# A linear-attention and feed-forward kernel: w3 @ w_out by row blocks, the weight loads moved and reordered, the last block made four units

## The chip, the core and the metric

The kernel runs on one core of a Trainium2 chip. A core has a matrix engine (TensorE, PE in the profile), a vector engine (VectorE, DVE), a scalar engine (ScalarE, ACT), GpSimd (POOL) and SyncE (SP), which issues transfers; 16 DMA engines move the data. Each engine works through its own queue in order. The metric is the device time of one execution in microseconds. Chances of "faster" and "slower" are meant against the median of the runs before.

## What is computed

```python
def _attn_ref(r, k, v, w, u):            # batch 4, heads 8, sequence 768, head_dim 48
    state = zeros((B, H, D, D)); y = zeros_like(r)
    for t in range(S):
        kt, vt, rt, wt = k[:, :, t], v[:, :, t], r[:, :, t], w[:, :, t]
        cur = einsum('bhd,bhe->bhde', u[None] * kt, vt)
        y[:, :, t] = einsum('bhd,bhde->bhe', rt, state + cur)
        state = wt[:, :, :, None] * state + einsum('bhd,bhe->bhde', kt, vt)
    return y

def _moe_ref(x, w1, w2, w3, w_out):      # x: y as 3072 tokens x 384; d_ff 1024
    h = (x @ w1) * (x @ w2) @ w3
    return h @ w_out
```

All inputs and the output are float32 in memory; the kernel multiplies in bfloat16. Since nothing stands between w3 and w_out, it forms w34 = w3 @ w_out (1024 x 384) once and uses that for the output.

## The kernel before

The 3072 tokens are 24 chunks (units) of 128: 4 batches with 6 chunks each. A chunk takes four loads of 192 KB (w, k, r, v, on SP's queue, line 237) and then the attention steps of `att(n)` (line 269): `ln` and the two cumulative sums `cs`, `ex`, the scaled k and r (`krt`), their transposes (`tr`, copied by `trs`), the chunk's contribution to the state (`kv`, `ts`, `pc`, `sbd`, `s_f`), the score matrix `m` with its two masked copies (`mb0`, `mb1`), `y`, and the diagonal term by way of `uk1`, `uk2`, `ds`, `yd`. `yb` adds the two, `yt` transposes and `xt` writes the chunk into `xT` of its block. `vb` casts v to bfloat16 on POOL. A trace names tiles, so that `uk1` and `uk2` both show as uk, `mb` as mbf, `ln` as lw.

The feed-forward works on blocks of chunks (`BLOCKS`, line 177): two blocks of two, four of four, and two of two at the end. For each of 8 column blocks `fi`, `a` and `b` (line 438) multiply w1 and w2 with xT, `as` copies a out of PSUM on ScalarE and `ab` multiplies it with b on VectorE. `o` (line 468) multiplies the product with w34, `os` copies it out, `st` stores. w34 comes from two steps: 8 times `wt` (8 transposes of w3, copied into the full transposed `w3T`, line 490) and then 8 times `wm` (line 500), which needs all eight copies; `wc` casts each result.

Every step is given to `Plan` (line 14) with its engine, an assumed length, its needs and the buffers that it takes and frees. `Plan._pass` walks through assumed time: of the ready steps the one that can start first on its engine goes next, and `rank` decides ties. The result is a fixed order, in which the instructions are issued; on the chip each engine keeps that order, whatever the real durations are. The plan knows loads of chunks at 1000 rows per us, and at 85 rows per us in the windows that it gives to weight loads. A "need" between a POOL load and an earlier POOL step is no wait on the chip, only a place in the queue.

Weights are loaded by POOL: w1 and w2 after `ld_r0`, w3 and w_out after `ld_v3` in the plan. Attention is put into the list of steps ahead of the feed-forward parts by a running count (`lead, every = 3, 4.1`).

Of the kernel before, what the change touches and what calls it, by code (L numbers as in the profile page):

```python
# [13 lines left out]
class Plan:  # L14
# [21 lines left out]
    def _pass(self, windows):  # L36
        end, eng_free, taken, owner, released = {}, {}, {}, {}, {}
        left = dict(self.steps)
        waiting = {n: sum(d not in end for d in s["needs"]) for n, s in left.items()}
        users = {}  # L40
        for n, s in left.items():
            for d in s["needs"]:
                users.setdefault(d, []).append(n)
        frees = {}
        for n, s in left.items():
            for o in s["free"]:
                frees[o] = frees.get(o, 0) + 1
        freed = {}
        ready = {n for n, c in waiting.items() if c == 0}
        order, ring, ring_free, big_free, new_windows, start = [], [], 0.0, 0.0, [], {}  # L50
        while left:
            best = {}
            for n in ready:
                s = left[n]
                t = eng_free.get(s["eng"], 0.0)
                for d in s["needs"]:
                    t = max(t, end[d] + (self.HOP if self.steps[d]["eng"] != s["eng"] else 0.0))
                ok = True
                for b in s["take"]:
                    i = taken.get(b, 0) - self.count[b]  # L60
                    if i >= 0:
                        o = owner[b, i]
                        if freed.get(o, 0) < frees[o]:
                            ok = False
                            break
                        t = max(t, released[o] + self.HOP)
                if not ok:
                    continue
                if s["rows"] and len(ring) >= 8:
                    t = max(t, ring[-8])  # L70
                best.setdefault(s["eng"], []).append((t, s["rank"], n))
            assert best, ("stuck", sorted(left)[:20])
            picks = []
            for e, c in best.items():
                t0 = min(c)[0]
                picks.append(min((max(t, t0), r, n) for t, r, n in c if t <= t0 + 1e-9))
            t, _, n = min(picks)
            s = left.pop(n)
            ready.discard(n)
            order.append(n)  # L80
            start[n] = t
            eng_free[s["eng"]] = t + s["length"]
            if s["rows"]:
                at, rows = max(t + 0.3, ring_free), s["rows"]
                while rows > 1e-6:
                    w = next((x for x in windows if x[0] <= at < x[1]), None)
                    nxt = w[1] if w else min([x[0] for x in windows if x[0] > at] + [1e9])
                    rate = 85.0 if w else 1000.0
                    d = min(rows / rate, nxt - at)
                    rows -= d * rate  # L90
                    at += d
                ring_free = at
                end[n] = at + 1.9
                ring.append(end[n])
            elif s["big"]:
                at = max(t + 2.0, big_free)
                big_free = at + s["big"]
                new_windows.append((at, big_free))
                end[n] = big_free + 1.5
            else:  # L100
                end[n] = t + s["length"] + s["lag"]
            for b in s["take"]:
                owner[b, taken.get(b, 0)] = n
                taken[b] = taken.get(b, 0) + 1
            for o in s["free"]:
                freed[o] = freed.get(o, 0) + 1
                released[o] = max(released.get(o, 0.0), end[n])
            for u in users.get(n, ()):
                waiting[u] -= 1
                if waiting[u] == 0:  # L110
                    ready.add(u)
        return order, new_windows, start, end
# [28 lines left out]
def kernel(  # L141
# [23 lines left out]
    P = 128  # L165
# [8 lines left out]
    TB = 512  # L174
    NU = B * NC
    NIN = 8
    BLOCKS = [(0, 2), (2, 4)] + [(n, n + 4) for n in range(4, NU - 4, 4)] + [(NU - 4, NU - 2), (NU - 2, NU)]
    NB = len(BLOCKS)

    consts = ctx.enter_context(tc.tile_pool(name="consts", bufs=1))  # L180
    wpool = ctx.enter_context(tc.tile_pool(name="weights", bufs=1))
# [32 lines left out]
    w2_bf = wpool.tile([P, DI, DFF], BF)  # L214
    w3_bf = wpool.tile([P, FI, DFF], BF)
    wo_bf = wpool.tile([P, FI, DM], BF)
    w3T = wpool.tile([P, FI, DFF], BF)
    w34 = wpool.tile([P, FI, DM], BF)

    NS = 3  # L220
# [6 lines left out]
    for i in range(NS):  # L227
# [2 lines left out]

    plan = Plan()
    plan.buffers(w_in=NIN, kr_in=NIN, v_in=NIN, lw=NS, krt=NS, sbd=NS, v_bf=3, e_sb=2, uk=2, ds=2, yd=3,
                 trs=2, mbf=2, pc=2, ts=2, s_f=2, y_bf=2, a_sb=3, o_sb=3, xT=3, abT=3, f=3, t=2, m=1, y=1)
    T = {}


    def load(n):
# [25 lines left out]

    def load_w(name, dst, ap, size, needs):
        plan.add(name, "POOL", 0.9, lambda: pool.dma_start(dst, ap.rearrange("(i p) f -> p i f", p=P)),
                 needs=needs, big=size, rank=-1)


    def att(n):
# [138 lines left out]
        if not last:  # L408
# [15 lines left out]
        A(f"uk2{n}", "POOL", 1.05, uk2, needs=[f"uk1{n}", f"ld_r{n}"], free=[f"ld_k{n}"])  # L424
        A(f"ds{n}", "DVE", 0.5, ds, needs=[f"uk2{n}"], take=["ds"], free=[f"uk1{n}"])
        A(f"yd{n}", "POOL", 0.82, yd, needs=[f"ds{n}", f"vb{n}"], take=["yd"], free=[f"ds{n}"])
        A(f"y{n}", "PE", 0.42, y, needs=[f"mb1{n}"] + ([f"sbd{n - 1}"] if c else []), take=["y"], lag=0.2,
          free=[f"mb0{n}", f"trs{n}", f"vb{n}"] + ([f"sbd{n - 1}"] if c else []))
        A(f"yb{n}", "DVE", 0.5, yb, needs=[f"y{n}", f"yd{n}"], take=["y_bf"], free=[f"y{n}", f"yd{n}"])
        A(f"yt{n}", "PE", 0.18, yt, needs=[f"yb{n}"], take=["t"], lag=0.2, free=[f"yb{n}"])  # L430
# [7 lines left out]
    def ffn_ab(j, fi):  # L438
# [14 lines left out]
        def mul():  # L453
# [3 lines left out]

        A = plan.add
        xs = [f"xt{n}" for n in range(lo, hi)]
        A(f"a{j}.{fi}", "PE", 0.65 * s, lambda: half("a", w1_bf), needs=xs + ["w1"], take=["f"], lag=0.2)  # L460
        A(f"b{j}.{fi}", "PE", 0.65 * s, lambda: half("b", w2_bf), needs=xs + ["w2", f"a{j}.{fi}"], take=["f"],
          lag=0.2, free=[f"xt{lo}"] if fi == FI - 1 else [])
        A(f"as{j}.{fi}", "ACT", 0.1 + 0.43 * s, a_cp, needs=[f"a{j}.{fi}"], take=["a_sb"], free=[f"a{j}.{fi}"])
        A(f"ab{j}.{fi}", "DVE", 0.1 + 0.53 * s, mul,
          needs=[f"as{j}.{fi}", f"b{j}.{fi}"] + ([f"ab{j}.0"] if fi else []), take=[] if fi else ["abT"],
          free=[f"as{j}.{fi}", f"b{j}.{fi}"])

    def ffn_out(j, t_):
        lo, hi = BLOCKS[j]
# [11 lines left out]
        def st():  # L481
# [2 lines left out]
        A = plan.add  # L484
        A(f"o{j}.{t_}", "PE", 1.3, o, needs=[f"ab{j}.{fi}" for fi in range(FI)] + [f"wc{fi}" for fi in range(FI)],
          take=["f"], lag=0.2, free=[f"ab{j}.0"] if t_ == hi - lo - 1 else [])
        A(f"os{j}.{t_}", "ACT", 0.43, os, needs=[f"o{j}.{t_}"], take=["o_sb"], free=[f"o{j}.{t_}"])
        A(f"st{j}.{t_}", "SP", 0.06, st, needs=[f"os{j}.{t_}"], free=[f"os{j}.{t_}"], rows=300, rank=-1)

    def w34_transpose(gi):  # L490
        def wt():
            t = T["wt", gi] = ps_f.tile([P, FI, P], BF, tag="f", name="wt")
            for fi in range(FI):
                pe.transpose(t[:, fi, :], w3_bf[:, fi, gi * P:(gi + 1) * P], I128)

        plan.add(f"wt{gi}", "PE", 0.46, wt, needs=["w3"], take=["f"], lag=0.2)
        plan.add(f"w3T{gi}", "DVE", 0.63, lambda: dve.tensor_copy(
            w3T[:, gi, :].rearrange("p (f q) -> p f q", q=P), T["wt", gi]), needs=[f"wt{gi}"], free=[f"wt{gi}"])

    def w34_mul(fi):  # L500
        def wm():
            t = T["wm", fi] = ps_f.tile([P, DM], F32, tag="f", name="wm")
            for gi in range(FI):
                pe.matmul(t, lhsT=w3T[:, gi, fi * P:(fi + 1) * P], rhs=wo_bf[:, gi, :],
                          start=(gi == 0), stop=(gi == FI - 1))

        plan.add(f"wm{fi}", "PE", 1.3, wm, needs=["wo"] + [f"w3T{gi}" for gi in range(FI)], take=["f"], lag=0.2)
        plan.add(f"wc{fi}", "ACT", 0.43, lambda: act.copy(w34[:, fi, :], T["wm", fi]), needs=[f"wm{fi}"],
                 free=[f"wm{fi}"])


    load(0)
    plan.add("ld_u", "SP", 0.06, lambda: sp.dma_start(u_bc, u.partition_broadcast(C)), rows=700)
    for n in range(1, NU):
        load(n)
    load_w("w1", w1_bf, moe_w1, 4.25, ["ld_r0"])
    load_w("w2", w2_bf, moe_w2, 4.25, ["w1"])
    load_w("w3", w3_bf, moe_w3, 11.4, ["w2", "ld_v3"])
    load_w("wo", wo_bf, moe_w_out, 5.0, ["w3"])
    plan.steps["w2"]["needs"], plan.steps["wo"]["needs"] = ["ld_r0"], ["ld_v3"]  # L520

    parts = []

    def add_ab(j):
        for fi in range(FI):
            parts.append((1.3 * (BLOCKS[j][1] - BLOCKS[j][0]) / 4, lambda fi=fi: ffn_ab(j, fi)))

# [1 line left out]
        for t in range(BLOCKS[j][1] - BLOCKS[j][0]):  # L529
            parts.append((1.3, lambda t=t: ffn_out(j, t)))  # L530

    add_ab(0)
    add_ab(1)
    for gi in range(FI):
        parts.append((0.45, lambda gi=gi: w34_transpose(gi)))
    for fi in range(FI):
        parts.append((1.3, lambda fi=fi: w34_mul(fi)))
    add_out(0)
    add_out(1)
    for j in range(2, NB):  # L540
        add_ab(j)
        add_out(j)

# [39 lines left out]
```

## Time and profile before

| | us |
|---|---|
| median of 10 runs | 201.72 (200.89 to 202.56) |
| the profiled execution | 201.54 |
| its span | 199.8 |
| PE busy | 169.5 |
| VectorE, ScalarE, GpSimd busy | 135.0, 110.8, 116.9 |

Busy time on PE contains the modelled ends of pipelined matmuls, so a busy PE can still be at less than its peak. In a timeline each row has the start, the time, the engine, the line, the operation with output and inputs, and in brackets how long the engine had been idle and what ended that. In a row of waits stand the total, the number and the longest. All calls go through one helper, so that nearly every row has line 136, and tiles tell the steps apart. q1 is the queue of SP's loads and stores, q0 that of POOL's weight loads.

### The profile page before, as it was taken

The page shows a single profiled execution, that of the slowest core. Times are in us where ns is not written, and L with a number is a line of the kernel's source. Part 1 is how long each engine was busy: PE and PEld are TensorE (multiplying, and loading weights), DVE is VectorE, ACT ScalarE, POOL GpSimd, SP SyncE. Part 2 cuts the span into 40 slices and gives each one's busy share as a digit, 9 for nine tenths or more (in the row PEclk, how much of TensorE's full clock was granted, in tenths as well). Part 3 has the DMA queues.
Part 4 walks back from the last instruction along what each step waited for, and adds up shares of the span by engine and source line. Part 5 has one row for each costly group of instructions (what it writes and reads, how often), then busy time and mean ns, then how long its engine had stood idle before and what let it go on. Part 6 is the DMA issues. An engine that isn't in the chain of part 4 may idle for free.

```text
span 199.8 us, 4553 instructions
## 1 busy us (share of the span) xinstructions
PE 169.5 (85%) x1720; PEld 107.6 (54%) x1720; DVE 135.0 (68%) x238; ACT 110.8 (55%) x213; POOL 116.9 (59%) x152
## 2 busy tenths in 40 slices
PE   0500578979999998999999898999999999999992
PEld 0300246768856665644566444465556555668771
DVE  5201656896798757868979799948896488734240
ACT  3301236765645765677485774775765675645441
POOL 8131896976159999999899978896244422000000
PEclk9999999999999999999999999999999999999999
DMA  6999999999989999999999999992001300022112
GB/s 118 175 199 179 197 186 191 198 202 186 184 162 194 154 196 190 199 231 193 197 189 212 219 195 190 177 223 86 3 0 39 121 0 3 0 80 82 39 41 79
DMA packets 106342, 28.54 MB, mean 143 GB/s; under 512 B 100304, under 2 KB 104528, under 8 KB 106320
## 3 DMA queue, kind: packets, MB, share of 16 engines
q1 hardware_dynamic: 103440, 23.80, 64.5%
q0 software_dynamic: 2880, 4.46, 12.7%
q8 instruction: 13, 0.21, 0.5%
q14 instruction: 9, 0.07, 0.1%
HBM read 27.98 MB, written 4.72 MB: 164 GB/s over the span
## 4 chain that ended last, share of the span: by engine, by line
PE 54%; DVE 14%; POOL 11%; DMA 7%; issue 6%; ACT 4%; SPq 2%; POOLq 0%; DVEq 0%; ACTq 0%
PE o_ps L136 13%; PE b L136 12%; PE a L136 12%; DMA w_in<-in_w_dram 7%; POOL uk L136 6%; PE tr L136 4%; DVE abT L136 3%; PE m L136 3%; DVE mbf L136 3%; PE cs L136 3%; PE y L136 3%; DVE krt L136 3%; PE kv L136 2%; POOL sbd L136 2%; SPq L136 2%
## 5 line engine op out<-in xcount | busy, mean ns | idle before, releaser
L136 PEld LDWEIGHTS <-w_bf 128*128 128x128 bf16 x448 | 39.9, 99 | 23.7 <-issue 3.8
L136 DVE TENSOR_TENSOR abT<-a_sb,b 128x256 bf16<-128x256 f32 (+1 forms) x64 | 34.1, 548 | 14.1 <-PE b L136 7.7
L136 PE MATMUL a<-xT,w_bf 128*128 128x256 bf16 (+1 forms) x192 | 39.9, 333 | 1.5 <-ACT xT L136 1.3
L136 PE MATMUL b<-xT,w_bf 128*128 128x256 bf16 (+1 forms) x192 | 40.3, 330 | 0.8 <-DVE abT L136 0.7
L136 ACT COPY a_sb<-a 128x256 f32<-128x256 f32 (+1 forms) x64 | 30.3, 481 | 18.4 <-PE a L136 16.1
L136 PE MATMUL o_ps<-w,abT 128*128 128x384 bf16 x192 | 34.7, 326 | 0.0
L136 DVE TENSOR_TENSOR mbf<-m,mask 128x512 bf16<-128x512 f32 x48 | 31.6, 681 | 3.4 <-PE m L136 3.4
L136 ACT COPY trs<-tr 128x1024 bf16<-128x1024 bf16 x24 | 24.3, 1013 | 15.3 <-PE tr L136 15.1
L136 DVE TENSOR_TENSOR krt<-kr_in,e_sb 128x768 bf16<-128x768 f32 x24 | 27.9, 1164 | 4.8 <-ACT e_sb L136 4.8
L136 POOL TENSOR_TENSOR uk<-kr_in,u_bc 128x384 f32<-128x384 f32 x24 | 25.4, 1059 | 7.8 <-DMA u_bc<-in_u_dram 4.7
L136 POOL TENSOR_TENSOR yd<-v_bf,ds 128x384 bf16<-128x384 bf16 x24 | 23.3, 973 | 8.4 <-DVE ds L136 5.8
L136 POOL TENSOR_TENSOR uk<-uk,kr_in 128x384 f32<-128x384 f32 x24 | 27.3, 1136 | 1.2
L136 ACT ACTIVATE e_sb<-cs 128x768 f32<-128x768 f32 x24 | 19.6, 816 | 12.4 <-PE cs L136 12.0
L136 PEld LDWEIGHTS <-krt 128*128 128x128 bf16 (+1 forms) x352 | 17.4, 109 | 13.0 <-DVE krt L136 7.5
L136 PEld LDWEIGHTS <-abT 128*128 128x128 bf16 x192 | 17.7, 97 | 10.8
L136 PE MATMUL tr<-I,krt 128*128 128x128 bf16 x192 | 16.0, 231 | 5.1 <-DVE krt L136 5.0
L136 PE MATMUL y<-v_bf,mbf 128*128 128x48 bf16 x192 | 9.8, 186 | 12.0 <-DVE mbf L136 11.9
L136 DVE TENSOR_REDUCE ds<-uk 128x8 f32<-128x384 f32 x24 | 13.1, 546 | 10.0 <-POOL uk L136 7.8
L136 ACT COPY o_sb<-o_ps 128x384 f32<-128x384 f32 x24 | 11.5, 479 | 14.2 <-PE o_ps L136 14.2
L136 ACT ACTIVATE lw<-w_in 128x384 bf16<-128x384 f32 x24 | 12.5, 524 | 12.1 <-DMA w_in<-in_w_dram 12.1
L136 POOL CAST v_bf<-v_in 128x384 bf16<-128x384 f32 x24 | 13.7, 572 | 8.8 <-DMA v_in<-in_v_dram 4.5
L136 DVE TENSOR_TENSOR y_bf<-y,yd 128x384 bf16<-128x384 f32 x24 | 13.2, 552 | 6.9 <-PE y L136 4.9
(95 smaller groups left out, 182.8 us busy)
## 6 DMA issues: line engine op xcount, KB each, us to landing
w_in<-in_w_dram SPq DMA_DIRECT2D x24, 192.0 KB, 4.5
kr_in<-in_k_dram SPq DMA_DIRECT2D x24, 192.0 KB, 4.5
kr_in<-in_r_dram SPq DMA_DIRECT2D x24, 192.0 KB, 4.6
v_in<-in_v_dram SPq DMA_DIRECT2D x24, 192.0 KB, 4.5
out_dram<-o_sb SPq DMA_DIRECT2D x24, 192.0 KB, 1.9
w_bf<-in_moe_w_dram POOLq DMA_DIRECT2D x1, 2048.0 KB, 16.5
w_bf<-in_moe_w_dram POOLq DMA_DIRECT2D x2, 768.0 KB, 11.7
wo_bf<-in_moe_w_out_dram POOLq DMA_DIRECT2D x1, 768.0 KB, 20.5
```

The costliest lines, as they stand in the source:

```text
L136: return self.tc.keep_in_program_order(f(*a, **k))
```

## The change

1. w1 and w2 are issued by POOL behind `vb1`, the cast of the second chunk's v; w_out and then w3, in two halves of four row blocks, directly behind them. Before, w1 and w2 came first of all and w3 before w_out.
2. w34 is made one row block at a time: `wt` transposes the eight pieces of one row block of w3, `wtc` copies them into one of two small w3T buffers, `wm` multiplies them with w_out, `wc` casts. The first four parts need the first half of w3 only.
3. The last two blocks of two chunks become one block of four.
4. In the plan, `as`, `ab` and `os` get rank -50 (before all attention steps in a tie); `a` needs the `b` before it; `y` needs `vb`; needs on the same engine no longer add the lag; a buffer can be freed under the name of its user and itself, so that PSUM and w3T of one `wt` are freed apart.

```diff
@@ Plan._pass
                 for d in s["needs"]:
-                    t = max(t, end[d] + (self.HOP if self.steps[d]["eng"] != s["eng"] else 0.0))
+                    if self.steps[d]["eng"] != s["eng"]:
+                        t = max(t, end[d] + self.HOP)
...
-                        o = owner[b, i]
-                        if freed.get(o, 0) < frees[o]:
+                        keys = [o for o in (owner[b, i], owner[b, i] + ":" + b) if o in frees]
+                        if any(freed.get(o, 0) < frees[o] for o in keys):
                             ok = False
                             break
-                        t = max(t, released[o] + self.HOP)
+                        t = max([t] + [released[o] + self.HOP for o in keys])
@@ sizes
-    BLOCKS = [(0, 2), (2, 4)] + [(n, n + 4) for n in range(4, NU - 4, 4)] + [(NU - 4, NU - 2), (NU - 2, NU)]
+    BLOCKS = [(0, 2), (2, 4)] + [(n, n + 4) for n in range(4, NU, 4)]
+    EARLY = 2
+    W3G = 4
...
-    w3T = wpool.tile([P, FI, DFF], BF)
...
+    EV = -50
@@ load_w
-                 needs=needs, big=size, rank=-1)
+                 needs=needs, big=size, rank=-100 + len(plan.steps) / 1000)
@@ att
-        A(f"y{n}", "PE", 0.42, y, needs=[f"mb1{n}"] + ([f"sbd{n - 1}"] if c else []), take=["y"], lag=0.2,
+        A(f"y{n}", "PE", 0.42, y, needs=[f"mb1{n}", f"vb{n}"] + ([f"sbd{n - 1}"] if c else []), take=["y"], lag=0.2,
@@ ffn_ab, ffn_out
-        A(f"a{j}.{fi}", "PE", 0.65 * s, lambda: half("a", w1_bf), needs=xs + ["w1"], take=["f"], lag=0.2)
+        before = [f"b{j}.{fi - 1}"] if fi else [f"b{j - 1}.{FI - 1}"] if j else []
+        A(f"a{j}.{fi}", "PE", 0.65 * s, lambda: half("a", w1_bf), needs=xs + ["w1"] + before, take=["f"], lag=0.2)
...
-        A(f"as{j}.{fi}", ..., free=[f"a{j}.{fi}"])
+        A(f"as{j}.{fi}", ..., free=[f"a{j}.{fi}"], rank=EV)
...
-          free=[f"as{j}.{fi}", f"b{j}.{fi}"])
+          free=[f"as{j}.{fi}", f"b{j}.{fi}"], rank=EV)
...
-        A(f"os{j}.{t_}", ..., free=[f"o{j}.{t_}"])
+        A(f"os{j}.{t_}", ..., free=[f"o{j}.{t_}"], rank=EV)
@@ w34_transpose and w34_mul become w34_part
+    def w34_part(fi):
         def wt():
-            t = T["wt", gi] = ps_f.tile([P, FI, P], BF, tag="f", name="wt")
-            for fi in range(FI):
-                pe.transpose(t[:, fi, :], w3_bf[:, fi, gi * P:(gi + 1) * P], I128)
+            t = T["wt", fi] = ps_f.tile([P, FI, P], BF, tag="f", name="wt")
+            for gi in range(FI):
+                pe.transpose(t[:, gi, :], w3_bf[:, fi, gi * P:(gi + 1) * P], I128)
+
+        def wtc():
+            t = T["w3T", fi] = work.tile([P, FI, P], BF, tag="w3T", name="w3T")
+            dve.tensor_copy(t, T["wt", fi])
...
-                pe.matmul(t, lhsT=w3T[:, gi, fi * P:(fi + 1) * P], rhs=wo_bf[:, gi, :],
+                pe.matmul(t, lhsT=T["w3T", fi][:, gi, :], rhs=wo_bf[:, gi, :],
...
+        A(f"wt{fi}", "PE", 0.46, wt, needs=[f"w3.{fi // W3G}"], take=["f", "w3T"], lag=0.2)
+        A(f"wtc{fi}", "DVE", 0.63, wtc, needs=[f"wt{fi}"], free=[f"wt{fi}:f"])
+        A(f"wm{fi}", "PE", 1.3, wm, needs=["wo", f"wtc{fi}"], take=["f"], lag=0.2, free=[f"wt{fi}:w3T"])
@@ loads
-    load_w("w1", w1_bf, moe_w1, 4.25, ["ld_r0"])
-    load_w("w2", w2_bf, moe_w2, 4.25, ["w1"])
-    load_w("w3", w3_bf, moe_w3, 11.4, ["w2", "ld_v3"])
-    load_w("wo", wo_bf, moe_w_out, 5.0, ["w3"])
-    plan.steps["w2"]["needs"], plan.steps["wo"]["needs"] = ["ld_r0"], ["ld_v3"]
+    AFTER1, AFTER2 = "vb1", "vb1"
+    load_w("w1", w1_bf, moe_w1, 4.25, [AFTER1])
+    load_w("w2", w2_bf, moe_w2, 4.25, [AFTER1])
+    load_w("wo", wo_bf, moe_w_out, 5.0, [AFTER2])
+    for g in range(FI // W3G):
+        load_w(f"w3.{g}", w3_bf[:, g * W3G:(g + 1) * W3G], moe_w3[g * W3G * P:(g + 1) * W3G * P], 1.43 * W3G, [AFTER2])
@@ order of the parts
-    add_ab(0)
-    add_ab(1)
-    for gi in range(FI):
-        parts.append((0.45, lambda gi=gi: w34_transpose(gi)))
+    for j in range(EARLY):
+        add_ab(j)
     for fi in range(FI):
-        parts.append((1.3, lambda fi=fi: w34_mul(fi)))
-    add_out(0)
-    add_out(1)
+        parts.append((1.75, lambda fi=fi: w34_part(fi)))
...
```

More of the change, by code (lines that the diff above doesn't have):

```diff
@@ L71, in _pass @@
                 best.setdefault(s["eng"], []).append((t, s["rank"], n))
-            assert best, ("stuck", sorted(left)[:20])
+            assert best, ("stuck", [(n, left[n]["take"]) for n in sorted(ready)])
             picks = []
@@ L232 @@
     plan.buffers(w_in=NIN, kr_in=NIN, v_in=NIN, lw=NS, krt=NS, sbd=NS, v_bf=3, e_sb=2, uk=2, ds=2, yd=3,
-                 trs=2, mbf=2, pc=2, ts=2, s_f=2, y_bf=2, a_sb=3, o_sb=3, xT=3, abT=3, f=3, t=2, m=1, y=1)
+                 trs=2, mbf=2, pc=2, ts=2, s_f=2, y_bf=2, a_sb=3, o_sb=3, xT=3, abT=3, w3T=2, f=3, t=2, m=1, y=1)
     T = {}
+    EV = -50
     def load(n):
@@ L459, in ffn_ab @@
         xs = [f"xt{n}" for n in range(lo, hi)]
-        A(f"a{j}.{fi}", "PE", 0.65 * s, lambda: half("a", w1_bf), needs=xs + ["w1"], take=["f"], lag=0.2)
+        before = [f"b{j}.{fi - 1}"] if fi else [f"b{j - 1}.{FI - 1}"] if j else []
+        A(f"a{j}.{fi}", "PE", 0.65 * s, lambda: half("a", w1_bf), needs=xs + ["w1"] + before, take=["f"], lag=0.2)
         A(f"b{j}.{fi}", "PE", 0.65 * s, lambda: half("b", w2_bf), needs=xs + ["w2", f"a{j}.{fi}"], take=["f"],
           lag=0.2, free=[f"xt{lo}"] if fi == FI - 1 else [])
-        A(f"as{j}.{fi}", "ACT", 0.1 + 0.43 * s, a_cp, needs=[f"a{j}.{fi}"], take=["a_sb"], free=[f"a{j}.{fi}"])
+        A(f"as{j}.{fi}", "ACT", 0.1 + 0.43 * s, a_cp, needs=[f"a{j}.{fi}"], take=["a_sb"], free=[f"a{j}.{fi}"], rank=EV)
         A(f"ab{j}.{fi}", "DVE", 0.1 + 0.53 * s, mul,
           needs=[f"as{j}.{fi}", f"b{j}.{fi}"] + ([f"ab{j}.0"] if fi else []), take=[] if fi else ["abT"],
-          free=[f"as{j}.{fi}", f"b{j}.{fi}"])
+          free=[f"as{j}.{fi}", f"b{j}.{fi}"], rank=EV)
     def ffn_out(j, t_):
@@ L486, in ffn_out @@
           take=["f"], lag=0.2, free=[f"ab{j}.0"] if t_ == hi - lo - 1 else [])
-        A(f"os{j}.{t_}", "ACT", 0.43, os, needs=[f"o{j}.{t_}"], take=["o_sb"], free=[f"o{j}.{t_}"])
+        A(f"os{j}.{t_}", "ACT", 0.43, os, needs=[f"o{j}.{t_}"], take=["o_sb"], free=[f"o{j}.{t_}"], rank=EV)
         A(f"st{j}.{t_}", "SP", 0.06, st, needs=[f"os{j}.{t_}"], free=[f"os{j}.{t_}"], rows=300, rank=-1)
-    def w34_transpose(gi):
+    def w34_part(fi):
         def wt():
-            t = T["wt", gi] = ps_f.tile([P, FI, P], BF, tag="f", name="wt")
-            for fi in range(FI):
-                pe.transpose(t[:, fi, :], w3_bf[:, fi, gi * P:(gi + 1) * P], I128)
[L496 to L500, printed above, removed]
+            t = T["wt", fi] = ps_f.tile([P, FI, P], BF, tag="f", name="wt")
[4 more added lines that the diff above has]
+            dve.tensor_copy(t, T["wt", fi])
         def wm():
@@ L503, in wm @@
             for gi in range(FI):
-                pe.matmul(t, lhsT=w3T[:, gi, fi * P:(fi + 1) * P], rhs=wo_bf[:, gi, :],
+                pe.matmul(t, lhsT=T["w3T", fi][:, gi, :], rhs=wo_bf[:, gi, :],
                           start=(gi == 0), stop=(gi == FI - 1))
-        plan.add(f"wm{fi}", "PE", 1.3, wm, needs=["wo"] + [f"w3T{gi}" for gi in range(FI)], take=["f"], lag=0.2)
-        plan.add(f"wc{fi}", "ACT", 0.43, lambda: act.copy(w34[:, fi, :], T["wm", fi]), needs=[f"wm{fi}"],
-                 free=[f"wm{fi}"])
+        A = plan.add
+        A(f"wt{fi}", "PE", 0.46, wt, needs=[f"w3.{fi // W3G}"], take=["f", "w3T"], lag=0.2)
+        A(f"wtc{fi}", "DVE", 0.63, wtc, needs=[f"wt{fi}"], free=[f"wt{fi}:f"])
+        A(f"wm{fi}", "PE", 1.3, wm, needs=["wo", f"wtc{fi}"], take=["f"], lag=0.2, free=[f"wt{fi}:w3T"])
+        A(f"wc{fi}", "ACT", 0.43, lambda: act.copy(w34[:, fi, :], T["wm", fi]), needs=[f"wm{fi}"],
+          free=[f"wm{fi}"])
     load(0)
@@ L530, in add_out @@
             parts.append((1.3, lambda t=t: ffn_out(j, t)))
-    add_ab(0)
-    add_ab(1)
-    for gi in range(FI):
-        parts.append((0.45, lambda gi=gi: w34_transpose(gi)))
+    for j in range(EARLY):
+        add_ab(j)
     for fi in range(FI):
-        parts.append((1.3, lambda fi=fi: w34_mul(fi)))
-    add_out(0)
-    add_out(1)
-    for j in range(2, NB):
+        parts.append((1.75, lambda fi=fi: w34_part(fi)))
+    for j in range(EARLY):
+        add_out(j)
+    for j in range(EARLY, NB):
         add_ab(j)
```

## The prediction

> **What bounds the kernel now.** I read the page's slices first, then TensorE's waits, the timeline of the first 45 us, and last the DMA landings. The slices:
>
> ```profile
> PE 169.5 (85%) x1720; PEld 107.6 (54%) x1720; DVE 135.0 (68%) x238; ACT 110.8 (55%) x213; POOL 116.9 (59%) x152
> PE   0500578979999998999999898999999999999992
> PEclk9999999999999999999999999999999999999999
> DMA  6999999999989999999999999992001300022112
> ```
>
> A slice is 5 us. TensorE (PE) is full from about 35 us to 196 us and nearly idle before, so the span is PE's work plus what PE loses at the start. The DMA row is full until 137 us, but PE runs 60 us longer on what has been loaded, so bandwidth counts only early. The waits say what the start loses:
>
> ```profile
> PE y L136 <- DVE mbf L136: 11.9, 6, 10.0
> PE tr L136 <- DVE krt L136: 5.0, 5, 1.9
> PE cs L136 <- ACT lw L136: 4.5, 1, 4.5
> ```
>
> One wait of 10.0 us, put down to VectorE's mask multiply. The timeline says what stood behind it:
>
> ```profile
> 3.52 1.71 POOL L136 DMA_DIRECT2D w_bf<-in_moe_w_dram  x2
> 6.93 7.82 SPq L136 DMA_DIRECT2D kr_in<-in_r_dram  x1
> 12.22 0.99 POOL L136 TENSOR_TENSOR uk<-kr_in,u_bc 128x384 f32<-128x384 f32 x1 [4.68 <-DMA u_bc<-in_u_dram]
> 18.38 0.52 ACT L136 ACTIVATE lw<-w_in 128x384 bf16<-128x384 f32 x1 [9.06 <-DMA w_in<-in_w_dram]
> 18.81 0.16 ACT L136 ACTIVATE pc<-kv 128x4 f32<-128x4 f32 x1
> 30.73 1.44 PE L136 MATMUL a<-xT,w_bf 128*128 128x256 bf16 x6 [0.74 <-ACT xT L136]
> 31.27 0.94 POOL L136 DMA_DIRECT2D w_bf<-in_moe_w_dram  x1
> 36.79 0.83 PE L136 MATMUL b<-xT,w_bf 128*128 128x256 bf16 x6
> 52.62 3.79 PE L136 MATMUL wt<-I,w_bf 128*128 128x128 bf16 x56
> ```
>
> w1 and w2 leave POOL at 3.5 us and share the engines with u and chunk 1. w of chunk 1, issued at 4.72, is used at 18.38; ScalarE has it queued ahead of pc of chunk 0, so chunk 0 stands still too. The first w1 matmul comes at 30.73 and waits for xT, not for weights. w3 leaves at 31.27, and its transposes come as a burst at 52.6.
>
> ```profile
> DMA to landing us min/median/max: 10.0/13.4/16.5
> wo_bf<-in_moe_w_out_dram POOLq DMA_DIRECT2D x1, 768.0 KB, 20.5
> ```
>
> The first line is the three w_bf loads: w1 lands at 3.5+10.0 = 13.5 us, w2 at 4.4+13.4 = 17.8, w3 at 31.3+16.5 = 47.8; w_out, behind w3, at 32.2+20.5 = 52.7.
>
> **PE's prices, warm**, from start-to-start in the timeline past 44 us: a chunk's attention 2.1 us (cs 0.33, tr 0.54, kv 0.36, m 0.33, y 0.37, yt 0.17); a and b of a block of two 5.3 (six matmuls of 256 in 0.66), of four 10.4 (three of 512 in 0.65); an output tile 1.3; w34 13.9 (eight times wt 0.44, wm 1.3). I call elapsed time minus finished work at these prices PE's loss. At 35.3 us PE has finished chunks 0 and 1 (4.2), cs, tr, kv of chunk 2 (1.2), cs of 3 (0.3) and 12 of block 0's 48 matmuls (1.3): 7.1, loss 28.2. At 83.9, where block 2's first a starts, another 43.1 is done in 48.6, loss 33.7. The whole work is 159 and PE ends at 196.1, loss 37. So 28 of 37 us lie in the first 35.
>
> **The change, part by part.**
>
> *w1 and w2 behind vb1.* Nothing waits by semaphore: the loads sit in POOL's queue behind chunk 1's v cast. u then lands at about 8 us (the same transfer stream without the weights; 12.2 now), pc of chunk 0 is planned before ln of chunk 1 since vb0 no longer stands behind the weight issues, and the 10.0 us wait goes. POOL then runs uk, uk, sbd, yd of chunk 0, uk and vb of chunk 1 (1.0+1.0+1.2+0.8+1.0+0.5, gaps 0.5): vb1 ends at about 14.0. All five weight issues follow at once, 5 x 0.89 = 4.4 us of POOL (four issues now, in two pairs). Queued behind them: uk2, sbd, yd of chunk 1; xT of chunk 1 is thereby at 23 us instead of 19, which w2 hides (below).
>
> *Landing.* Data starts 1.7 us after issue, so 15.7. How fast? w3 brought 2.1 MB (as bfloat16) in about 14.3 us, 147 KB/us; w_out 0.79 MB in 4.9, 160; w1 and w2 1.57 MB in 11.6, 136. From 10 to 18 us q0 moved 1.08 MB and q1 0.56. The Trainium skill ("DMA: Bandwidth & Descriptors", queues, rings and completion order) says an engine alternates between queues packet by packet, a packet being some 9 to 17 descriptors. With 1550-byte pieces against 192-byte ones (the page's bytes per packet), q1 would keep a ninth and weights get 8/9 of the 205 KB/us of both, 182; q1 kept a third. By the rule w3's first half would land at 35 us, by the trace, at 150, at 15.7 + 3.41 MB/150 + 0.8 = 39.2. I take the trace. w1 then lands near 22, w2 27, w_out 32, the second half 46.
>
> *What PE does meanwhile.* Chunks 0 to 2 are loaded by 16 us (one load per 1.0 us in SP's rows from 20 to 31 us), so three chunks of attention (6.3) and cs of 3 (0.3) are done by 27; block 0 (5.3) from 27 to about 34.5, its first part at half speed. What stands next in PE's queue? The planner lets chunk loads crawl at 85 rows/us beside weights (the trace has 2908 packets in 8 us, 364), so it takes r of chunk 3 for later than w3's first half, and puts the first wt before tr of chunk 3. So PE stands at wt from 34.5 to 39.2 with chunk 3 ready behind it; VectorE likewise, krt behind the wt copy. At 39.2 PE has finished 11.9: loss 27.3.
>
> *Clock.* After the 10 us hole eight tr took 1.03 us, later 0.61, and six a 1.44 at 30.73, later 0.82, while PEclk reads 9 throughout. The Trainium skill ("TensorE: Matmul & The Clock Gate", the HAM clock gate) has this: after an idle window of about 3.4 us PE runs at half rate until a busy one has passed. That speaks against this change, which makes a second hole of 4.7 us: 3.4 us at half rate is 1.7. By the granted-clock row it is 0. I take 1.7, as the durations do show two speeds: loss 29.0.
>
> *w34 by row block.* Same 64 transposes, 64 matmuls, 8 copies of 0.68, 8 casts of 0.48. The burst goes: 56 wt took 3.79 and a wait of 0.26 where 3.1 would do (1.0 back). Waits for yt and xT at 43 to 44 us (1.1) go too, as w34 fills them. The present loses 5.5 from 35.3 to 83.9; without these 3.4. So to the same work the loss is 29.0+3.4 = 32.4 against 33.7: **-1.3 us**. The second half (46 us) is not waited for, since four parts with chunk 3 take PE to 50. The two w3T buffers hide behind a wm of 1.3, the copy being 0.68.
>
> *Evictions first (EV), a and b in strict order.* No instruction added, only order on ScalarE and VectorE. From 84 us PE loses 3.5, so the gain is at most 2; the opposite, attention pushed back, I bound by +2 (twice the largest wait there, 0.79 of tr for krt, and some repeats). I take 0. The planner's accounting fixes also only change order.
>
> *Last block of four.* The present pair pays 0.70 per six matmuls of 256: 11.2 us; the block of four 10.4: -0.8. But now nothing of it can start before xT of chunk 23; now yt of 23 comes at 180.5, exactly when the earlier outputs are done, with six matmuls of the pair filling in. Without these 0.7 us and with the step yt to xT to a (0.74 in the row of 30.73) PE waits about 0.8. Sum 0, ends -0.8 and +1.5. The last output, its copy and store stay.
>
> *SP.* Stores of blocks 0 and 1 move up before later loads in SP's queue; with eight chunks of input buffers and loads a chunk or more ahead, I cost it at nothing; uncovered, it would be the wait for an output, 1 to 4 us.
>
> **Sum.** -1.3 + 0 + 0. The profiled execution took 201.54 us, 1.74 outside its span of 199.8, and lies 0.2 under the median 201.72. Forecast 200.4.
>
> **Rivals.**
>
> *Slower: PE stands longer at the first wt.* Same queue, but w3's first half late. The balance tips where it lands at 39.2 + 1.3 = 40.5; each us later costs one. At 136 KB/us (the row of w1 and w2) and vb1 1.5 us late it lands 42.3 to 43: 203.5 to 204.5, and with the tail's and evictions' bad ends 205. For it: the in-order queue and an early load rate that is the lowest of the three. Against: w3 and w_out went faster with q1 as full. Chance 0.38.
>
> *More gain: weights land as by the packet rule or at w2's pace* (4.3 us behind w1, 183 KB/us). First half at 35, no hole, no cold clock: -4 more and -1.7, less what PE can't use: 196.5 to 198. Chance 0.15.
>
> *No difference within 0.3%* (0.6 us, about what measuring this kernel can tell): the start only trades a hole at 10 to 20 us for holes at 24 to 27 and 35 to 39. 201.7, chance 0.12. This would also be the change not doing what it says: w1's matmuls start at 27 to 28 instead of 30.7, little for loads moved by 10 us.
>
> **Numbers.** The likeliest, a gain of 0.6 to 3 us, has 0.35; with the larger gain faster has 0.50, same 0.12, slower 0.38. The likeliest's own range is 198.7 to 201.1. Both signs hold much, so the range runs from within the large gain to within the late landing: 197.0 to 204.8.
>
> **To look for.** Right: no 10 us wait at y; pc of chunk 0 near 9.5; five POOL issues from 14; b's first matmul near 27; PE idle before the first wt, which starts near 39 at half speed; w34 through by 56; block 2's a near 83. Wrong: the wt before 36 or after 41; tr of chunk 3 ahead of it; a hole over 1.5 us before the last block; PE waits past 84 us adding to over 5.

## The result, and the profile after

The changed kernel takes 199.14 us (median; before, measured beside it, 201.54): the ratio is 0.9895, 95% interval 0.9874 to 0.9917. The forecast was 200.4, 197.0 to 204.8. The ratio and its interval are taken from the runs in the fast state alone, so the ratio is not quite the quotient of the two medians. The span fell from 199.8 to 197.4 us.

The slices of the page after, PE's busy tenths, granted clock and transfers in 40 slices of 4.9 us:

```profile
PE   0548479399999899999999799999999999989992
PEclk9999999969999999999999999999999999999998
DMA  6999999999999999999999999992002200031013
```

PE now works from the second slice on. It has a new hole in the eighth (a 3), with a slow clock just behind it (the 6 in PEclk). PE's longest waits after, in total, times and longest:

```profile
PE cs L137 <- ACT lw L137: 5.9, 2, 4.6
PE tr L137 <- DVE krt L137: 3.9, 5, 1.9
PE wt L137 <- DMA w_bf<-in_moe_w_dram: 3.1, 1, 3.1
PE yt L137 <- DVE y_bf L137: 2.0, 1, 2.0
PE y L137 <- DVE mbf L137: 1.5, 2, 1.3
```

The 10.0 us wait at y is gone. In its place stands the wait of the first wt for w3, 3.1 us. The timeline after, first POOL, then PE (start, time, operation, idle time before):

```profile
13.36 0.51 POOL L137 CAST v_bf<-v_in 128x384 bf16<-128x384 f32 x1
13.81 1.70 POOL L137 DMA_DIRECT2D w_bf<-in_moe_w_dram  x2
15.50 0.92 POOL L137 DMA_DIRECT2D wo_bf<-in_moe_w_out_dram  x1
16.42 1.51 POOL L137 DMA_DIRECT2D w_bf<-in_moe_w_dram  x2
36.03 0.99 POOL L137 TENSOR_TENSOR uk<-uk,kr_in 128x384 f32<-128x384 f32 x1 [5.61 <-DMA kr_in<-in_r_dram]
44.31 0.51 POOL L137 CAST v_bf<-v_in 128x384 bf16<-128x384 f32 x1 [7.29 <-DMA v_in<-in_v_dram]
...
27.23 0.82 PE L137 MATMUL b<-xT,w_bf 128*128 128x256 bf16 x3 [1.05 <-DMA w_bf<-in_moe_w_dram]
34.64 0.49 PE L137 MATMUL b<-xT,w_bf 128*128 128x256 bf16 x3
38.25 1.07 PE L137 MATMUL wt<-I,w_bf 128*128 128x128 bf16 x16 [3.12 <-DMA w_bf<-in_moe_w_dram]
39.66 2.74 PE L137 MATMUL wm<-wo_bf,w3T 128*128 128x384 bf16 x8 [0.34 <-DVE w3T L137]
42.19 0.87 PE L137 MATMUL tr<-I,krt 128*128 128x128 bf16 x8
43.35 1.46 PE L137 MATMUL wm<-wo_bf,w3T 128*128 128x384 bf16 x8
177.91 0.81 PE L137 MATMUL a<-xT,w_bf 128*128 128x512 bf16 x3 [0.82 <-ACT xT L137]
```

vb1 ends at 13.9, all weights are issued by 17.9, w2 is there at 27.2 and w3's first half at 38.2. Two rows are not as forecast: r and v of chunk 3 come at 36.0 and 44.3. So when PE came to the first wt, at 35, the chunk was not ready behind it. At the end PE waits 0.8 us for xT of chunk 23.

PE's loss, by the prediction's own prices, with the matmuls of each tile counted up to each time:

| at us | 20 | 35 | 45 | 60 | 80 | 100 | 140 | 170 | last matmul |
|---|---|---|---|---|---|---|---|---|---|
| before | 18.4 | 28.2 | 30.3 | 32.2 | 34.1 | 35.1 | 38.1 | 38.9 | 196.1 us |
| after | 14.9 | 23.2 | 28.4 | 29.2 | 30.8 | 32.8 | 34.9 | 35.8 | 193.6 us |
| won | 3.5 | 5.0 | 1.9 | 3.0 | 3.3 | 2.3 | 3.2 | 3.1 | 2.5 |

Of the 5.0 us that are won by 35, three are given back by 45, in the hole and its slow clock. What is won at 80 is about what remains at 170.

### The profile page after: what moved, and what is told of

Read it like the earlier page. It is cut to its first block, busy times and chain, and to the rows that moved or that the text cites. A ratio compares the mean times of both kernels' runs of the same rounds, so it can differ in the third digit from the quotient of the medians.

```text
span 197.4 us, 4420 instructions
## 1 busy us (share of the span) xinstructions
PE 171.6 (87%) x1672; PEld 104.9 (53%) x1672; DVE 135.8 (69%) x230; ACT 109.4 (55%) x205; POOL 115.6 (59%) x153
## 4 chain that ended last, share of the span: by engine, by line
PE 40%; POOL 28%; DMA 16%; issue 5%; DVE 5%; ACT 3%; SPq 1%; POOLq 0%; ACTq 0%
POOL uk L137 13%; DMA w_bf<-in_moe_w_dram 11%; PE o_ps L137 11%; PE a L137 8%; PE b L137 8%; POOL yd L137 5%; POOL sbd L137 5%; POOL v_bf L137 4%; PE wm L137 3%; DMA kr_in<-in_k_dram 2%; PE tr L137 2%; DMA u_bc<-in_u_dram 2%; PE y L137 2%; DVE krt L137 2%; PE kv L137 2%
## 5 line engine op out<-in xcount | busy, mean ns | idle before, releaser
L137 PEld LDWEIGHTS <-w_bf 128*128 128x128 bf16 x400 | 35.9, 100 | 31.3 <-DMA w_bf<-in_moe_w_dram 4.9
L137 DVE TENSOR_TENSOR abT<-a_sb,b 128x512 bf16<-128x512 f32 (+1 forms) x56 | 33.9, 606 | 16.0 <-PE b L137 13.1
L137 PE MATMUL a<-xT,w_bf 128*128 128x512 bf16 (+1 forms) x168 | 41.9, 360 | 1.1 <-ACT xT L137 0.8
L137 PE MATMUL b<-xT,w_bf 128*128 128x512 bf16 (+1 forms) x168 | 41.7, 359 | 1.1 <-DMA w_bf<-in_moe_w_dram 1.1
L137 ACT COPY a_sb<-a 128x512 f32<-128x512 f32 (+1 forms) x56 | 29.3, 527 | 23.3 <-PE a L137 23.1
L137 DVE TENSOR_TENSOR krt<-kr_in,e_sb 128x768 bf16<-128x768 f32 x24 | 29.2, 1219 | 5.3 <-ACT e_sb L137 5.2
L137 POOL TENSOR_TENSOR uk<-uk,kr_in 128x384 f32<-128x384 f32 x24 | 26.0, 1082 | 6.7 <-DMA kr_in<-in_r_dram 5.6
L137 PEld LDWEIGHTS <-abT 128*128 128x128 bf16 x192 | 17.6, 97 | 11.2
L137 POOL CAST v_bf<-v_in 128x384 bf16<-128x384 f32 x24 | 14.9, 622 | 13.5 <-DMA v_in<-in_v_dram 10.6
L137 PEld LDWEIGHTS <-trs 48*128 48x128 bf16 (+1 forms) x272 | 11.6, 99 | 8.9 <-issue 2.5
L137 ACT COPY xT<-yt 128x384 bf16<-128x384 bf16 x24 | 11.6, 482 | 7.7 <-PE yt L137 7.7
```

Of the source, the lines that this page charges most:

```text
L137: return self.tc.keep_in_program_order(f(*a, **k))
```

## The experiments

Ratios are to the kernel before, measured beside each kernel on the same chip. The changed kernel itself, measured once more beside the kernels with half of w3 and with quarters, gave 0.989 (0.9862 to 0.9917), and is called the control:

> The changed kernel itself, run on the same chip beside these three, as the level to compare them with: 0.9895.

**The parts undone one at a time.** First the loads as before, all else changed:

```diff
-    load_w("w1", ..., [AFTER1]); load_w("w2", ..., [AFTER1]); load_w("wo", ..., [AFTER2]); w3.g: [AFTER2]
+    load_w("w1", ..., ["ld_r0"]); load_w("w2", ..., ["ld_r0"]); w3.g: ["w2", "ld_v3"]; load_w("wo", ..., ["ld_v3"])
```

> The changed kernel with its weight loads placed as before (w1, w2 when r of chunk 0 is loaded; w3 in its two halves and then w_out when v of chunk 3 is). Theory 'loads': the gain is the attention of chunks 0 to 2 done before the weights, so the 10 us wait at y of chunk 0 returns and the ratio to the kernel before goes from 0.99 to 0.998 or more. Rival 'rest': w34 by row blocks, evictions first and the block of four carry the gain; then 0.988 to 0.993 though the 10 us wait is back.

Measured 0.998 (0.9965 to 0.9995), the first theory's number. PE's waits there:

```profile
PE y L137 <- DVE mbf L137: 10.5, 5, 9.4
PE tr L137 <- DVE krt L137: 5.4, 5, 1.9
```

The long wait at y is back. With the rest of the change in place, the moved loads are worth 0.9 of the 1.1%; the rest without them (row blocks, halves, evictions first, the last block) 0.2%. Next the other way round, the kernel before with the moved loads and w3 whole:

```diff
+    load_w("w1", ..., ["vb1"]); load_w("w2", ..., ["vb1"]); load_w("wo", ..., ["vb1"]); load_w("w3", w3_bf, moe_w3, 11.4, ["vb1"])
-    needs=xs + ["w1"]            # a
+    needs=xs + ["w1"] + before   # and vb as a need of y; the loads ranked as in the changed kernel; the kr tile is made by ld_k or ld_r, whichever is planned first
```

> The kernel before with only the loads moved: w1, w2, w_out, w3 (in one piece) behind vb1, and the plan needs without which this order can't be planned (a after the b before it, y after vb). w34 still in two stages, two blocks of two at the end. Theory 'loads': faster by 1 us or so, 0.993 to 0.997, with a longer hole before the first wt, as whole w3 lands at 44 us. Rival: without the halves PE stands 6 us longer at wt and the move alone is slower, 1.005 to 1.02.

Measured 1.0202 (1.0179 to 1.0225): slower, as the rival said, at the upper end of its size. Its PE timeline shows the rival's mechanism, with the first wt at 43 us, five later than in the changed kernel:

```profile
36.57 0.62 PE L136 MATMUL tr<-I,krt 128*128 128x128 bf16 x8 [2.55 <-DVE krt L136]
43.22 3.59 PE L136 MATMUL wt<-I,w_bf 128*128 128x128 bf16 x32 [4.32 <-DMA w_bf<-in_moe_w_dram]
```

The changed kernel with w3 in one piece says the same from the other side:

```diff
-    W3G = 4
+    W3G = 8
```

> The changed kernel with w3 loaded in one piece (W3G = 8). Theory: the first wt can start only when all of w3 is there, 44 us instead of 38, PE stands 6 us more unless the plan finds attention for it, which has no data: ratio 0.999 to 1.02. Rival: the halves are worth nothing since the plan fills the time with block 1: 0.989.

Measured 1.0197 (1.0154 to 1.024), at the top of the theory's range. PE waits 3.73 us for krt of chunk 3 and then 3.38 for w3, and its wt run slow (16 take 1.89 us instead of 1.07):

```profile
37.74 1.04 PE L137 MATMUL tr<-I,krt 128*128 128x128 bf16 x8 [3.73 <-DVE krt L137]
43.87 1.89 PE L137 MATMUL wt<-I,w_bf 128*128 128x128 bf16 x16 [3.38 <-DMA w_bf<-in_moe_w_dram]
```

So the move alone costs 2%, the rest without the move brings 0.2%, and both together win 1.1%. Weights back to back starve the chunks (v of chunk 3 takes 28 us to land, below), and the first half of w3 is what PE can work on then.

Then w3 in quarters:

```diff
-    W3G = 4
+    W3G = 2
```

> The changed kernel with w3 in four quarters (W3G = 2): two more issues on POOL, 1.6 us, and the first wt can start 3 us earlier, when block 0 is just done, so no hole and no slow clock. Theory 'loads bind until 58 us': PE is only ahead for a while, 0.988 to 0.991, as with the transposes in the hole. Rival: a real gain of the hole and the clock, 0.978 to 0.984.

Measured 0.9923 (0.9894 to 0.9951), near the first theory's number and no better than two halves. Its first wt starts at 36.25 after a wait of 0.59, and the wm behind it run at full speed (16 in 2.77 us); the hole is gone and nothing is gained. One thing speaks against a clean reading: block 0 starts 0.9 us later here (26.25 for 25.38), with two more weight issues on POOL ahead of chunk 1's last steps.

**Evictions and the last block.** Without the rank:

```diff
-        A(f"as{j}.{fi}", ..., rank=EV)      # also ab, os
+        A(f"as{j}.{fi}", ...)
```

> The changed kernel without rank -50 on as, ab and os. Forecast's step: evictions first are worth 0, so 0.989 as the changed kernel. Rival: the about 1 us that the change gains more than forecast between 60 and 140 us comes from it, then 0.994 to 0.996 with PE waits past 60 us up by 1 us.

Measured 0.9907 (0.9878 to 0.9935): not to be told from the changed kernel within 0.3%. With the last four chunks as two blocks:

```diff
-    BLOCKS = [(0, 2), (2, 4)] + [(n, n + 4) for n in range(4, NU, 4)]
+    BLOCKS = [(0, 2), (2, 4)] + [(n, n + 4) for n in range(4, NU - 4, 4)] + [(NU - 4, NU - 2), (NU - 2, NU)]
```

> The changed kernel with the last four chunks as two blocks of two; nothing else in the order moves. Forecast's step: the block of four saves 0.8 us of matmul time and loses 0.8 waiting for xT of chunk 23, so 0.989, no difference. Rival: the wait is lost anyway and the merge is worth its 0.8 us: 0.993. Other rival: the wait is the larger: 0.987.

Measured 0.9899 (0.9865 to 0.9933): no difference either, and its timeline lists no wait of PE in the last 30 us. The interval (0.7 us to each side) doesn't settle whether 0.8 us are won and lost again, or neither.

**The hole and the clock.** PE gets work in the hole that needs no load:

```diff
         t = T["wt", fi] = ps_f.tile([P, FI, P], BF, tag="f", name="wt")
+        for i in range(40 if fi == 0 else 0):
+            pe.transpose(t[:, i % FI, :], I128, I128)
```

> The changed kernel with 40 more transposes of the identity, put ahead of the first wt into its PSUM tile, so that PE has about 2.2 us of work in its 3.1 us wait for w3. Theory 'clock': the hole makes eight wm take 2.74 us instead of 1.46 and eight tr 0.87 instead of 0.61, some 1.5 us; filled, they run at full speed and the time falls by 0.8 to 1.5 us: ratio 0.982 to 0.986. Rival: PE is held by chunk 3's loads next (v of chunk 3 lands at 44 us) or the slow rows have another cause: 0.989.

Measured 0.9907 (0.9872 to 0.9943): no gain, the rival's number. Yet its PE timeline shows the first theory's mechanism at work:

```profile
34.22 2.39 PE L137 MATMUL wt<-I 128*128 128x128 bf16 x40
37.09 1.07 PE L137 MATMUL wt<-I,w_bf 128*128 128x128 bf16 x16 [0.48 <-DMA w_bf<-in_moe_w_dram]
38.50 1.48 PE L137 MATMUL wm<-wo_bf,w3T 128*128 128x384 bf16 x8 [0.34 <-DVE w3T L137]
58.38 0.49 PE L137 MATMUL a<-xT,w_bf 128*128 128x256 bf16 x3 [1.39 <-ACT a_sb L137]
```

Eight wm take 1.48 us instead of 2.74, and m of chunk 3 comes at 42.10 instead of 44.74: PE is 2.64 us ahead. But at 58.38 PE waits 1.39 us for a copy on ScalarE, and that one stands behind the load of a chunk's w:

```profile
57.54 0.52 ACT L137 ACTIVATE lw<-w_in 128x384 bf16<-128x384 f32 x1 [2.12 <-DMA w_in<-in_w_dram]
```

The matmul that waits there starts at 59.53 in the changed kernel, so that 1.15 us of the lead are left. The starts of other matmuls that both kernels have show the rest go later: 0.7 us are left at 105, 0.1 at 134. Up to there loads still hold POOL up in both kernels, at the k loads of four chunks between 95 and 128 us. The last of these waits, first in the changed kernel, then with the transposes:

```profile
127.20 0.99 POOL L137 TENSOR_TENSOR uk<-kr_in,u_bc 128x384 f32<-128x384 f32 x1 [1.31 <-DMA kr_in<-in_k_dram]
127.61 1.00 POOL L137 TENSOR_TENSOR uk<-kr_in,u_bc 128x384 f32<-128x384 f32 x1 [1.92 <-DMA kr_in<-in_k_dram]
```

So the loads may have taken the lead back. To test that, the second half of w3 is left out, with and without the 40 transposes (the half is 0.5 M elements, 2.1 of the 8.9 MB that the weight loads read; with it goes one issue of about 0.8 us on POOL):

```diff
-        plan.add(name, "POOL", 0.9, lambda: pool.dma_start(dst, ...), ...)
+        plan.add(name, "POOL", 0.9, lambda: name != "w3.1" and pool.dma_start(dst, ...), ...)
-                pe.transpose(t[:, gi, :], w3_bf[:, fi, gi * P:(gi + 1) * P], I128)
+                pe.transpose(t[:, gi, :], w3_bf[:, fi % W3G, gi * P:(gi + 1) * P], I128)
```

> The changed kernel in the same order, but the second half of w3 is never loaded, and the last four parts of w34 transpose the first half again: 0.5 M of 8.9 MB weight reads less, some 6 us of transfer at 169 KB/us. Theory 'loads': from 38 to 58 us chunk loads queue behind weights, so 6 us less of them ends the waits for w of chunks and for v of chunk 3, but the hole before wt with its slow clock stays: 0.982 to 0.987. Rival: loads don't bind after the hole: 0.9895.

> The same without the second half of w3, and with the 40 transposes that keep PE busy before the first wt. In the kernel that had only the transposes, PE was 2.7 us ahead at 50 us and lost it at 58 us, at ScalarE's wait for w of chunk 7. Theory 'the loads took back what the full clock had given': without that half the 1.5 to 2.5 us stay, so 0.972 to 0.980, that much below the kernel without the transposes. Rival: what was won is lost elsewhere in any case: no difference from it.

Measured 0.9856 (0.9826 to 0.9887) without the transposes and 0.9794 (0.9769 to 0.982) with them. Fewer loads without a filled hole gain 0.7 us against the control (the intervals overlap). With fewer loads the same 40 transposes win 1.3 us, with all loads nothing. The rival is refuted and the theory holds in kind; its size, 1.5 to 2.5 us, was a little high. In the profiled executions of these two the one with transposes is 0.77 us ahead at 41 us and still 0.77 at the last outputs, and in neither does POOL wait for a load between 48 and 140 us. The PE rows of the second kernel run through where the one with all loads waited:

```profile
57.17 0.49 PE L137 MATMUL b<-xT,w_bf 128*128 128x256 bf16 x3
57.56 0.49 PE L137 MATMUL a<-xT,w_bf 128*128 128x256 bf16 x3
57.91 0.49 PE L137 MATMUL b<-xT,w_bf 128*128 128x256 bf16 x3
```

**Was chunk 3 there?** The plan believes 300 rows per us for chunk loads beside weights:

```diff
-                    rate = 85.0 if w else 1000.0
+                    rate = 300.0 if w else 1000.0
```

> The changed kernel with the plan's rate for chunk loads beside weights at 300 rows per us instead of 85 (and the tile of k and r made by whichever load is planned first). The forecast took 364 from the trace and said that chunk 3 is ready behind the first wt: then the attention of chunk 3 goes into the hole, 0.980 to 0.987. Rival: beside the weights the loads really get 85 to 155 rows per us, v of chunk 3 lands at 44 us, and a plan that believes 300 puts PE, POOL and VectorE at waits for chunk 3: 1.00 or more.

Measured 1.0453 (1.0412 to 1.0494), the worst of all. Its waits:

```profile
PE tr L137 <- DVE krt L137: 14.2, 5, 11.2
PE kv L137 <- POOL v_bf L137: 2.7, 1, 2.7
```

The plan sends PE to tr of chunk 3 ahead of all of block 0 but its first a, and PE stands 11.2 us there, since r of chunk 3 is not loaded. The transfers of the changed kernel between 18 and 40 us, while weights flow without a break, show why (packets, MB, busy share; below, the last columns are size and us to landing):

```profile
q0 software_dynamic: 2576, 3.83, 95.9%
q1 hardware_dynamic: 2542, 0.48, 20.0%
...
v_in<-in_v_dram SPq DMA_DIRECT2D x1, 192.0 KB, 28.1
w_in<-in_w_dram SPq DMA_DIRECT2D x1, 192.0 KB, 25.7
```

2542 packets in 22 us are 116 rows per us and 11% of the bytes of the two queues (the weights counted as the bfloat16 that is written), and v of chunk 3 took 28.1 us to land.

**Weights apart.** w_out and w3 behind vb3:

```diff
-    AFTER1, AFTER2 = "vb1", "vb1"
+    AFTER1, AFTER2 = "vb1", "vb3"
```

> The changed kernel with w_out and w3 issued behind vb3 instead of vb1 (w1 and w2 stay behind vb1). Theory: chunks 2 and 3 load between the weights, block 1 takes the place of w34 in the hole, PE has work from 27 to 50 us without the wait at wt: 0.980 to 0.988. Rival: w3 then lands at 50 us or later, and without w34 PE lacks work from 35 to 50 us, as only chunks 0 to 4 are there: 0.992 to 1.0.

Measured 0.9957 (0.9935 to 0.9978), inside the rival's numbers. But the rival's mechanism, a PE without work from 35 to 50 us, does not show: its first wt starts at 46.89 without a wait, as block 1 stands before it, and its longest PE wait from 27 to 50 us is 1.46, for y_bf. Its profiled execution has the changed kernel's span (197.5), its median is 200.0. Why it is slower than the changed kernel by 0.6% was not found. No version tried that computes everything beats the changed kernel.

## Why the prediction was right or wrong

- *vb1, the issues, the landings.* Right: vb1 14.0 (measured 13.9), w2 27 (27.2), w_out 32 (15.5 + 17.0 = 32.5); w3's first half 39.2 (38.2), second 46 (17.2 + 26.8 = 44.0).
- *The share of the queues.* This step failed. I took a third for q1 from the window of 10 to 18 us. By 16 us 1.55 of the 1.57 MB of w1 and w2 had been moved, so that the last two us of the window were the chunk loads' alone. Inside, from 11 to 15 us in the kernel before, q1 has 9% of the bytes, in as many packets:

```profile
q0 software_dynamic: 373, 0.73, 96.2%
q1 hardware_dynamic: 372, 0.07, 16.1%
```

In the changed kernel it has 11% from 18 to 40 us, again packet for packet (above). That is the ninth which I had worked out from the Trainium skill's rule ("DMA: Bandwidth & Descriptors", queues, rings and completion order: an engine changes queues packet by packet) and then set aside. Weights flowed at 174 KB/us instead of 150 (182 by the rule). That the first half of w3 still came within 1 us of the forecast was luck. An estimate from q0's bytes: its 3.41 MB had been moved by 36.5 us instead of 38.4. The faster flow alone would have made it 35.3, but up to 18 us only 0.23 MB had come. Then wt started 1.7 us after the last byte, where I had put 0.8.
- *"With chunk 3 ready behind it".* Wrong: r landed at 36.0, v at 44.3. The place of wt ahead of tr cost little: with r at 36.0 and a krt of 1.0 us, tr (0.5) is all that could have gone into the hole before 38.25.
- *"Bandwidth counts only early".* Wrong too, though no term of the sum hung on it: POOL waits for chunk loads as late as 127 us. The filled hole left the loads where they were (the last chunk load is issued at 128.7 us in the changed kernel, at 129.0 with the transposes, at 124.9 with them and half of w3).
- *The clock.* Right in kind and nearly in size. Eight wm took 2.53 us to the next start instead of 1.30 and eight tr 0.71 instead of 0.45: 1.5 us for a forecast of 1.7. The Trainium skill's rule ("TensorE: Matmul & The Clock Gate", the HAM clock gate) holds in kind: a slow spell follows the hole, from 39.7 to about 42.9. Its idle window of about 3.4 us is not to be taken strictly: waits at wt of 3.12 us here and 2.84 in the kernel with two last blocks were enough. Nor is the start of the spell fixed: the first 16 wt after the hole ran at full speed here (1.07 us) and slow in the control (1.89), which is the same kernel. One reading behind the term was no proof: in the kernel before, eight tr took 1.03 us at 7.23 too, ahead of the 10 us hole, and in the changed kernel, without that hole, PE is at half speed until 32 us.
- *The start's sum.* Its direction was right, its size wrong: -1.3 us to 84, measured -3.3 at 80. The terms: the loss when the slow clock ends 28.4 for 29.0 (first half 1 us earlier); the loss from there to 80, 2.4 for 3.4; and before, 34.1 for 33.7. These make 2.0.
- *Evictions first.* 0, and no more was found.
- *The last block.* The wait for xT of chunk 23 was 0.8 by forecast and 0.82 in the trace. By the table PE's lead shrinks from 3.1 to 2.5 us after 170 us, so +0.6 for a forecast of 0; with 0.8 saved on matmuls, 1.4 must have been lost, and the wait is 0.82 of that.
- *The sum.* -3.3 to 80, +0.2 to 170, +0.6 after it: -2.5 us, which the last matmul shows (193.6 for 196.1). The forecast was -1.3: the direction and the path were right, and the size was half.
- *The signs.* w34 was through at 70.6 us instead of 56, as the plan puts block 1 between its parts; the table shows no jump in PE's loss there. Block 2's first a came at 79.8 instead of 83. PE's listed waits past 84 us add up to 2.6, under the 5 that was to be a sign of being wrong.
- *The rivals.* The slower one didn't come about: the half landed at 38.2, before the 40.5 from which it was to decide. With whole w3 its mechanism comes true, at a little over its price: 1.3 us faster at 39.2 and a us for each us makes 2.7 and 3.4 slower at 43.2 and 43.9; measured 4.1 and 4.0. (By its own terms the late landing is 41.6 to 43.1, not 42.3 to 43.) The large-gain rival wanted weights that land at 35, which no kernel here had. But the two that gave PE work in the hole gained nothing of its 4 to 6 us, as the loads then bind.

## What to carry to other kernels

An engine that idles while everything loads is a question of order: first what starts the long chain, then the weights, cut so that the first piece is enough to work on. Moving the loads and cutting them paid only together. Before filling a hole, ask what the engine meets next: here PE was 2.6 us earlier and met loads that came at their own pace. And read a shared rate from the middle of the shared stretch, where both queues have work: 2 us of one queue alone, in a window of 8, turned a ninth into a third.

## What the runs showed of the hardware that was not expected

- While both had work, POOL's weight loads and SP's chunk loads moved as many packets: 2576 and 2542 in the changed kernel from 18 to 40 us, 373 and 372 in the kernel before from 11 to 15. POOL's packets are larger (3.83 MB in 2576 is 1.5 KB each, against 0.2), so that SP's queue kept 11 and 9% of the bytes.
- The granted clock shows some slow spells and not others. It reads 0.50 at 40 us, where wm take twice their time, and in the control at 37 us, where wt do. But eight tr at 14.75 us took 1.06 us, about half speed, in a stretch listed with 1.00. PE's busy time first, the clock third from the end; changed kernel, then control:

```profile
15.00:16.00 1.00, 1.00 (x16) 0.80 (x14) 0.26 (x2) 0.95 (x2) 1.00 (x2) 1.00 1.52 194
40.00:41.00 1.00, 1.00 (x5) 0.50 (x4) 1.00 (x3) 0.00 (x0) 0.00 (x0) 0.50 1.12 201
37.00:38.00 1.00, 0.78 (x8) 0.79 (x9) 0.00 (x0) 0.00 (x0) 0.00 (x0) 0.50 1.12 201
```
